# Batch 0 by GpSimd's casting queue, u turned by transposing transfers in five batches, and a new order of the whole list

## The chip, the cores and the metric

The kernel runs on one core of a Trainium2 chip. The metric is the device time of one execution in microseconds. Before the change the median of three runs is 213.06 us (212.74 to 214.03).

## What is computed

The program joins two blocks. The first is a linear attention per head, with a norm over the head's 64 columns; the second mixes tokens and channels with a phase.

```python
kv  = einsum('bhsd,bhse->bhde', k, v)          # 8 batches, 8 heads, 576 rows, 64 columns
o   = einsum('bhsd,bhde->bhse', q, kv)
x   = o / sqrt(mean(o*o, -1) + 1e-6) * g_norm   # then [batch, 576, 512]
th  = x @ w_theta
y   = w_tok_r @ (x * cos(th)) + w_tok_i @ (x * sin(th))
u   = x + y
out = u + maximum(u @ w_ch, 0)                  # float32, 8 x 576 x 512
```

## The kernel before, in words

Each batch has 576 rows. Four tiles of 128 rows (the index j from 0 to 3, called full) and a tail of 64 rows (j = 4, called half-size) make one batch; where a tail is worked on, the two halves of its 512 columns lie on the two halves of the partitions, so it is a tile of 128 x 256. Everything that goes into a matmul is f16, everything that comes out is f32 in PSUM.

`plan()` writes down all tasks of the eight batches. The string `TURNS` is an order over them: each number is a task, and the engines get their instructions in just this order. A letter behind a number moves the task to another engine (A is ACT, D is DVE). A word like `f14` puts 14 filling transposes ahead of the next tile of PSUM, `r20` puts 20 idle matmuls there. Since each engine takes its instructions in order, a task that waits holds up all that stands behind it on its engine, and this is so for the queues of transfers that SP and POOL issue.

For one batch the tasks are these, with the engine that mostly has them:

- `ldm`, `ldt` load k and v (the full rows, the tails), `lq`, `lqe` load q. From batch 1 on they go by POOL's queue, whose transfers turn f32 into f16 on the way, into one of three buffers for each of k, v and q. Batch 0's k and v go as f32 into two buffers of their own (`stage`), k by SP's queue and v by ACT's, in halves of four heads. Two `hold` instructions (L329) on POOL copy one number out of these, so that POOL issues q and the weights only after they are in. `kv_of` (L273) says which buffers a batch uses.
- `kv` (PE), `ko` (ACT or DVE): the 64 x 64 products of k and v, copied into a block-diagonal tile `kbd`.
- q must be turned. For batches 0 and 1 and for all tails `qt` does it on PE and `qo` copies the result out of PSUM; for the full tiles of batches 2 to 7 `qd` (L396) does it by a transposing transfer that SP issues, two for each batch, each from 128 x 1024 to 128 x 8 x 128.
- `raw` (PE) multiplies; `sq` (ACT), `ss` (DVE) and `rt` (POOL, a power of -0.5, L444) make the norm; `x` (DVE) applies it.
- `xt` (PE), `xo` (mostly ACT) turn x; `th` (PE) makes the angle. `pt` (ACT), `arg` (DVE, L511) reduce it to one period, `abs` (DVE, L518) takes its absolute value, `sin` and `cos` (ACT, L526 and L532) follow; the cosine is the one that reads the absolute value. `z` (DVE) multiplies.
- `y`, `ye` (PE, L565 and L574) mix the tokens over nine blocks of the turned token weights `wT`; `us` (DVE, L579) adds x and leaves u turned, channels on partitions, in one of three parts of `uTb`. The tail has `um`, `ug`, `ute`, `uoe`.
- `v` (PE) multiplies the turned u with `wch`. The last sum needs u with rows on partitions: `ut` (L606) turns each full tile back on PE by four transposes, `uo` (L609) copies it from PSUM into `ur`, and `fin` (DVE, L620) makes u + max(v, 0). `st`, `ste` store it by SP's queue.

The weights come once at the start: `lw`, `lwe` (token weights, both parts into the room that `uTb` takes later), `lwth`, `lwch`; `wt` turns the token weights on PE, `wo` copies them out, `wth` scales w_theta. Before all tasks DVE clears the tails of the buffers for k and v and both `kbd`, POOL makes the identity that PE's idle matmuls and transposes need, and PE runs 20 idle matmuls.

Of the kernel before, what the change touches and what calls it, by code (L numbers as in the profile page):

```python
# [40 lines left out]
def plan():  # L41
# [14 lines left out]
    for hh in range(2):  # L56
        add("lqe", "POOL", 0, hh)
    add("hold", "POOL", "k", 0, 0)
    add("hold", "POOL", "k", 0, HH)
# [5 lines left out]
    add("lwth", "POOL")  # L65
# [7 lines left out]
    for b in range(B):  # L73
        if b:
            for t in "kv":
                add("ldm", LOAD[t], t, b, 0, H)
                add("ldt", LOAD[t], t, b)
            add("lq", "POOL", b, 0, H)
            for hh in range(2):
                add("lqe", "POOL", b, hh)  # L80
# [51 lines left out]
4 1 5 0 2 18 16 17 r20 f3 44 45 3 f4 48 49 46A 47 51 50 11 10 6 7 13 12 f14 52 53D f2 54 55 56 21 19  # L132
9 8 59 66 67D 60 f2 61 73 15 14 180 57 62 63 74D 64 178 179 58 f19 34 38 35 68 39A 69 65 30 31A 70
87 75 f10 80 76 23 81 24A 25D 88D 77 26 22 71 78 72 96 97 27A 181 89 82 98 36 79 105 83 90 37 99 84
91 106D 85 182 184 320 183 92 r1 32 114 107 33D 86 100 123 124D 101 93 115 94 102 28 116 95 29D 103
108 104 125 109 42 40 134 117 126 127 111 129 118 119 43 110 120 121 112 41 122 113 128 185 186 187
136 188 190 130 189 135 f9 191 192 198 139 219 193 194 318 317 322 319 131 199D 141 321 146 144 200
195 201 220 140 205 20 196 149 151 132 133 330 331 202 203 323 206D 197 204 153 207 145 137 212 208
# [6 lines left out]
751 362 291 346 460 349 354 461A 355 273 370 462 293D 371 159 174 169 350 363 365 364 366 356 351  # L145
752 357 278 854 988 586 584 587 855 274 283 386 279 377 372 358 373 387D 374 375 367 288 395 284 465
# [3 lines left out]
298 308 420 502 495 590 482 479 483 419 408 496 591 413 592 487 418 593 503 406 720 718 484 594A 885  # L150
488 504 595 519 411 497 489 505 520D 490 716 498 499 983 510 598 407 416 506 423 424 491 500 599 507
# [544 lines left out]
```

## Time and profile before

| | |
|---|---|
| runs | 212.74, 213.06, 214.03 us |
| the profiled execution | 213.28 us |
| its span, first to last instruction | 211.5 us |
| busy: PE, DVE, ACT, POOL | 193.5, 175.2, 135.7, 112.7 us |
| granted clock of TensorE over the span | 0.992 |
| chain that ended last, by engine | PE 47%, DMA 17%, DVE 11%, ACT 7%, POOL 6% |
| DMA queues, share of 16 engines | POOL's casting queue 60.1%, SP's 27.0%, ACT's 1.8% |
| read from HBM, written to it | 33.10 MB, 9.44 MB |

The table is read with two cautions. The ends of matmuls are modelled, so PE's share says when it had something in flight and not how densely it ran. And the share of an engine over the span mixes three stages: a start in which batch 0 and the weights come in, a middle in which several batches overlap, and an end in which only the last batches' products and stores are left.

### The profile page before, as it was taken

What the parts mean: (1) busy time and instruction counts of PE and PEld (TensorE: products, weight loads), DVE (VectorE), ACT (ScalarE), POOL (GpSimd) and SP (SyncE); (2) the same over time, 40 slices, a digit from 0 to 9 for tenths busy, and PEclk for the clock granted to TensorE, in tenths of its full rate; (3) what the DMA queues carried; (4) which work ended last, traced back from release to release, by engine and by line L of the source; (5) the groups of instructions that cost most, each with busy time, mean ns of one, the idle gap of its engine ahead of it and who ended that gap; (6) DMA issues with size and microseconds to landing.
All of it is one profiled execution on the core that took longest, in us unless ns stands there. A gap on an engine that the chain in (4) does not pass through costs nothing.

```text
span 211.5 us, 4732 instructions
## 1 busy us (share of the span) xinstructions
PE 193.5 (91%) x1838; PEld 110.7 (52%) x1838; DVE 175.2 (83%) x358; ACT 135.7 (64%) x271; POOL 112.7 (53%) x116
## 2 busy tenths in 40 slices
PE   7977899999896999999998989799999999999970
PEld 2555557556444565655564565446555556454530
DVE  7016698978997999999998999989999999786660
ACT  2032999469985799599945898658973984570020
POOL 1299898397595899597393643575237310100010
PEclk9999999999999999999999999999999999999996
DMA  5999999994999999999999996999111042214341
GB/s 160 287 139 271 212 184 182 196 192 82 79 183 156 183 228 170 158 219 193 135 119 219 205 183 136 217 144 153 50 54 50 0 120 67 66 50 132 94 173 52
DMA packets 57702, 31.15 MB, mean 147 GB/s; under 512 B 26832, under 2 KB 53072, under 8 KB 57680
## 3 DMA queue, kind: packets, MB, share of 16 engines
q0 software_dynamic: 35888, 15.88, 60.1%
q1 hardware_dynamic: 20208, 13.80, 27.0%
q10 hardware_dynamic: 1584, 1.18, 1.8%
q8 instruction: 14, 0.23, 0.4%
q14 instruction: 8, 0.07, 0.1%
HBM read 33.10 MB, written 9.44 MB: 201 GB/s over the span
## 4 chain that ended last, share of the span: by engine, by line
PE 47%; DMA 17%; DVE 11%; ACT 7%; issue 7%; POOL 6%; POOLq 0%; DVEq 0%; ACTq 0%
PE y L565 17%; DMA k<-in_k_dram 11%; PE v L483 9%; PE th L483 8%; POOL rt L444 4%; DMA uTb<-in_moe_w_tok_r_dram 4%; PE ups L380 3%; DMA qDD<-qh 3%; PE ye L574 2%; DVE ss L438 2%; PE xps L380 2%; PE raw L409 2%; DVE ot L624 2%; ACT sc L532 1%; PE th L490 1%
## 5 line engine op out<-in xcount | busy, mean ns | idle before, releaser
L444 POOL TENSOR_TENSOR rt<-ss,mhalf 128x8 f32<-128x8 f32 x32 | 53.5, 1674 | 35.7 <-DVE ss L438 35.4
L565 PE MATMUL y<-wT,zm 128*128 128x512 f16 x256 | 62.8, 379 | 0.2 <-DVE ot L624 0.2
L565 PEld LDWEIGHTS <-zm 128*128 128x128 f16 x256 | 23.6, 98 | 23.7 <-issue 0.5
L483 PE MATMUL th<-wth,xTb 128*128 128x512 f16 x128 | 32.2, 379 | 0.1
L483 PE MATMUL v<-wch,uTb 128*128 128x512 f16 x128 | 31.9, 379 | 0.0
L429 ACT ACTIVATE sqb<-raw 128x512 f32<-128x512 f32 x32 | 19.1, 598 | 13.9 <-PE raw L409 13.7
L579 DVE SCALAR_TENSOR_TENSOR uTb<-y,gcol,xTb 128x512 f16<-128x512 f32 x32 | 23.4, 743 | 3.0 <-PE y L565 2.9
L438 DVE TENSOR_REDUCE ss<-sqb 128x8 f32<-128x520 f32 x32 | 21.9, 686 | 4.0 <-ACT sqb L429 4.0
L265 ACT COPY ur<-ups 128x512 f16<-128x512 f16 x28 | 16.2, 585 | 13.8 <-PE ups L380 13.8
L526 ACT ACTIVATE sc<-arg 128x512 f16<-128x512 f32 x32 | 20.2, 632 | 6.6 <-DVE arg L511 6.5
L532 ACT ACTIVATE sc<-arg,quarter 128x512 f16<-128x512 f32 x32 | 22.7, 719 | 2.5 <-DVE arg L518 2.5
L456 DVE TENSOR_TENSOR x<-raw,rt 128x512 f16<-128x512 f32 x32 | 21.9, 683 | 2.9 <-POOL rt L444 2.6
L506 ACT ACTIVATE pt<-th 128x512 f32<-128x512 f32 x32 | 18.9, 599 | 7.9 <-PE th L483 7.6
L593 POOL TENSOR_TENSOR uge<-ue,g 128x256 f32<-128x256 f16 x8 | 5.9, 736 | 32.6 <-DVE ue L587 32.6
L624 DVE SCALAR_TENSOR_TENSOR ot<-v,ur 128x512 f32<-128x512 f32 x32 | 21.6, 682 | 1.9 <-PE v L483 1.2
L511 DVE SCALAR_TENSOR_TENSOR arg<-pt,th 128x512 f32<-128x512 f32 x32 | 21.4, 679 | 1.9 <-ACT pt L506 1.7
L540 DVE TENSOR_TENSOR zm<-x,sc 128x1024 f16<-128x1024 f16 x32 | 22.0, 696 | 0.5 <-ACT sc L532 0.4
L267 ACT ACTIVATE xTb<-xps,gcol 128x512 f16<-128x512 f16 x23 | 15.6, 686 | 3.4 <-PE xps L380 3.0
L265 ACT CAST kbd<-kv 64x256 f16<-64x256 f32 (+1 forms) x28 | 9.6, 343 | 12.4 <-PE kv L363 11.1
L483 PEld LDWEIGHTS <-xTb 128*128 128x128 f16 x128 | 11.5, 97 | 11.5 <-issue 0.6
L483 PEld LDWEIGHTS <-uTb 128*128 128x128 f16 x128 | 11.4, 98 | 10.0 <-issue 0.6
L444 POOL TENSOR_TENSOR rte<-sse,mhalf 128x4 f32<-128x4 f32 x8 | 8.6, 1073 | 12.1 <-DVE sse L438 12.1
(101 smaller groups left out, 321.9 us busy)
## 6 DMA issues: line engine op xcount, KB each, us to landing
out_dram<-ot SPq DMA_DIRECT2D x32, 256.0 KB, 2.5
v<-in_v_dram POOLq DMA_DIRECT2D x7, 512.0 KB, 8.6
k<-in_k_dram POOLq DMA_DIRECT2D x7, 512.0 KB, 9.3
qh<-in_q_dram POOLq DMA_DIRECT2D x7, 512.0 KB, 8.6
stage<-in_v_dram ACTq DMA_DIRECT2D x2, 512.0 KB, 8.6
stage<-in_k_dram SPq DMA_DIRECT2D x2, 512.0 KB, 5.4
zm<-in_moe_w_theta_dram POOLq DMA_DIRECT2D x1, 1024.0 KB, 10.3
out_dram<-ote SPq DMA_DIRECT2D x8, 128.0 KB
```

The source lines that it names most:

```text
L265: nc.scalar.copy(out=dst, in_=src)
L438: nc.vector.reduce_sum(out=ss[:], in_=live.pop(("sq", b, j))[:], axis=AXX)
L444: nc.gpsimd.tensor_tensor(out=rt[:], in0=live.pop(("ss", b, j))[:], in1=mhalf[:, 0:h], op=ALU.pow)
L456: nc.vector.tensor_tensor(out=live["xp", b, p][:, :, a * HC:(a + 1) * HC].rearrange("p t (h e) -> p h t e", e=D), in0=r[:].rearrange("p (h ...
L483: nc.tensor.matmul(t[:], lhs(kc), w[:, kc, :], start=(kc == 0), stop=(kc == NKC - 1))
L511: nc.vector.scalar_tensor_tensor(out=arg[:, 0, :], in0=live.pop(("pt", b, j))[:], scalar=MAGIC, in1=live.pop(("th", b, j))[:], op0=ALU.sub ...
L526: nc.scalar.activation(out=sc[:, 1, :], in_=live["arg", b, j][:, 0, :], func=AFT.Sin, bias=0.0, scale=-TURN * SHRINK,)
L532: nc.scalar.activation(out=live["sc", b, j][:, 0, :], in_=live.pop(("arg", b, j))[:, 1, :], func=AFT.Sin, bias=quarter[:], scale=-TURN * S ...
L540: nc.vector.tensor_tensor(out=zm[b % NZ][:, j, :, :], in0=x.unsqueeze(1).broadcast_to((P, 2, C)), in1=sc[:], op=ALU.mult,)
L565: nc.tensor.matmul(t[:], r[:, c * P:(c + 1) * P], wT[:, w, 0:SM], start=(w == 0), stop=(w == 2 * NJ))
L579: nc.vector.scalar_tensor_tensor(out=uTb[:, b % NUT, c, :].rearrange("p (j t) -> p j t", j=NJ), in0=live.pop(("y", b, c))[:].rearrange("p ...
L624: nc.vector.scalar_tensor_tensor(out=ot[:], in0=live.pop(("v", b, j))[:], scalar=0.0, in1=u[:], op0=ALU.max, op1=ALU.add,)
```

## The change

- Batch 0's k and v come by POOL's casting queue as f16, in the same halves, as the first things that POOL issues; `stage`, SP's and ACT's loads and the `hold` instructions are gone. The identity and the constants of -0.5 become a task (`ident`) that stands behind the first four loads.
- k and v have four buffers each instead of three.
- u of batches 2 to 6 (`UD`) is turned back by transposing transfers that SP issues (`ud`), each for two of the four full tiles, into one of two buffers `urd`; for these batches `ut` and `uo` are gone. `uTb` is laid out by tile first, so that a pair of tiles is one run of 1024 columns. A transfer needs all four `us` of its batch.
- q's tail comes in one transfer for each batch with 64 rows on partitions instead of two on 128; PE turns it by four transposes of 64 rows instead of two of 128.
- ACT can take `abs`. With the new marks in `TURNS` 24 of the 32 full and 4 of the 8 half-size ones are its; in exchange DVE has three more `ko`, six half-size `qo` more and two full ones fewer, and one more of `wo`, `wth`.
- `TURNS` is new from end to end, with 13 idle matmuls at the start instead of 20.

```diff
-NSTG, NKV, NQ, NZ, NXT, NUT = 2, 3, 3, 3, 2, 3
+NSTG, NKV, NQ, NZ, NXT, NUT = 0, 4, 3, 3, 2, 3
+NURD = 2
+UD = (2, 3, 4, 5, 6)
-F32 = (0,)
+F32 = ()
...
-        add("ldm", "SP", "k", 0, lo, HH)
-        add("ldm", "ACT", "v", 0, lo, HH)
-    add("ldt", "SP", "k", 0)
-    add("ldt", "ACT", "v", 0)
+        for t in "kv":
+            add("ldm", LOAD[t], t, 0, lo, HH)
+    for t in "kv":
+        add("ldt", LOAD[t], t, 0)
...
-    add("hold", "POOL", "k", 0, 0)
-    add("hold", "POOL", "k", 0, HH)
+    add("ident", "POOL")
...
-            if j < NJ:
+            if b in UD and j % 2 == 0 and j < NJ:
+                add("ud", "SP", b, j // 2)
+            elif j < NJ and b not in UD:
                 add("ut", "PE", b, j)
                 add("uo", "ACT", b, j)
...
-4 1 5 0 2 18 16 17 r20 f3 44 45 3 f4 48 49 46A 47 51 50 11 10 6 7 13 12 f14 52 53D f2 54 55 56 21 19
+0 5 1 4 9 r13 f2 42 43 44A 15 16 14 19 6 2 3 45 f11 50 7 11 8 10 64 51D f1 52 53 54 f19 46 47 49D 48
...
-    qe = many(NQ, [P, HH, D], FP16, "qe")
+    qe = many(NQ, [TL, H, D], FP16, "qe")
...
-    uTb = const.tile([P, NUT, NKC, SM], FP16, name="uTb")
+    uTb = const.tile([P, NUT, NJ, NKC, P], FP16, name="uTb")
...
-    def e_lqe(eng, b, hh):
-        nc.gpsimd.dma_start(
-            out=qe[b % NQ][hh * TL:(hh + 1) * TL, :, :],
-            in_=q[b, hh * HH:(hh + 1) * HH, SM:S, :].rearrange("h s d -> s h d"),
-        )
+    def e_lqe(eng, b):
+        nc.gpsimd.dma_start(out=qe[b % NQ][:], in_=q[b, :, SM:S, :].rearrange("h s d -> s h d"))
...
+    def e_ident(eng):
+        make_identity(nc, ident)
+        nc.gpsimd.memset(mhalf[:], -0.5)
...
-        else:
-            turned("qps", lambda i: qe[b % NQ][:, 2 * i:2 * i + 2, :], NHP // 2, ("qp", b, j))
+            return
+        t = live["qp", b, j] = bank([P, NHP // 2, P], FP16, "tr", 2, "qps")
+        for i in range(NHP):
+            hh, p = divmod(i, 2)
+            nc.tensor.transpose(
+                t[:, p, hh * TL:(hh + 1) * TL], qe[b % NQ][:, 2 * i:2 * i + 2, :], ident[0:TL, 0:TL]
+            )
...
     def e_abs(eng, b, j):
         arg = live["arg", b, j]
+        if eng == "ACT":
+            nc.scalar.activation(out=arg[:, 1, :], in_=arg[:, 0, :], func=AFT.Abs)
+            return
...
-            out=uTb[:, b % NUT, c, :].rearrange("p (j t) -> p j t", j=NJ),
+            out=uTb[:, b % NUT, :, c, :],
...
+    def e_ud(eng, b, p):
+        src = uTb[:, b % NUT, 2 * p:2 * p + 2, :, :]
+        d = wk("urd", [P, 2 * NKC, P], FP16, NURD)
+        nc.sync.dma_start_transpose(out=d[:], in_=src.rearrange("p j k t -> p (j k t)"))
+        for i in range(2):
+            live["ur", b, 2 * p + i] = d[:, NKC * i:NKC * (i + 1), :].rearrange("p k c -> p (k c)")
```

The order changes everywhere, so three places are shown. The first is POOL's opening; `k_64`, `v_68` and `qh_72` are batch 0's buffers, `uTb` holds the token weights at this time. Before:

```order
masks.py:197 MEMSET ident 128x128
masks.py:199 ISA
masks.py:199 AFFINE_SELECT ident<-ident 128x128
L649 MEMSET mhalf 128x8
L329 COPY gate<-stage_64 1x1 x2
L293 DMA qh_72<-in_q_dram 128x4x256 x2
L311 DMA uTb<-in_moe_w_tok_r_dram 64x576
L305 DMA uTb<-in_moe_w_tok_r_dram 128x2304
```

Now:

```order
L279 DMA k_64<-in_k_dram 128x4x256
L285 DMA v_68<-in_v_dram 64x8x64
L279 DMA v_68<-in_v_dram 128x4x256
L285 DMA k_64<-in_k_dram 64x8x64
masks.py:197 MEMSET ident 128x128
masks.py:199 ISA
masks.py:199 AFFINE_SELECT ident<-ident 128x128
L330 MEMSET mhalf 128x8
L292 DMA qh_72<-in_q_dram 128x4x256
```

The loads of batch 0 have taken the place of the two copies that held POOL, and the identity has moved behind four of them.

The second place is DVE from the last `us` of batch 3 on (the numbers behind a tile's name tell one use from another). Before:

```order
L579 SCALAR_TENSOR_TENSOR uTb_90<-y_2012,gcol_102,xTb1_87 128x512
L511 SCALAR_TENSOR_TENSOR arg_2075<-pt_2073,th_2027 128x512
L540 TENSOR_TENSOR zm1_81<-x_1689,sc_2038 128x1024
L511 SCALAR_TENSOR_TENSOR arg_2119<-pt_2108,th_2047 128x512
L624 SCALAR_TENSOR_TENSOR ot_2121<-v_2068,ur_1808 128x512
L456 TENSOR_TENSOR x_2045<-raw_2007,rt_2110 128x4x2x64
L624 SCALAR_TENSOR_TENSOR ote_2124<-v_2089,uge_2032 128x256
L438 TENSOR_REDUCE ss_2126<-sqb1_97 128x8
L271 TENSOR_SCALAR xTb1_87<-xps_2160,gcol_102 128x512
L518 TENSOR_SCALAR arg_2119<-arg_2119 128x512
L518 TENSOR_SCALAR arg_2075<-arg_2075 128x512
L511 SCALAR_TENSOR_TENSOR arge_2194<-pte_2173,th_2141 128x256
```

Now:

```order
L588 SCALAR_TENSOR_TENSOR uTb_90<-y_1995,gcol_102,xTb1_87 128x4x128
L517 SCALAR_TENSOR_TENSOR arg_2056<-pt_2039,th_2028 128x512
L462 TENSOR_TENSOR x_2073<-raw_2013,rt_2047 128x4x2x64
L517 SCALAR_TENSOR_TENSOR arg_2075<-pt_2070,th_2050 128x512
L444 TENSOR_REDUCE sse_2150<-sqe0_98 128x4
L517 SCALAR_TENSOR_TENSOR arge_2154<-pte_2148,th_2077 128x256
L641 SCALAR_TENSOR_TENSOR ote_2156<-v_2128,uge_2000 128x256
L270 TENSOR_SCALAR xTb1_87<-xps_2065,gcol_102 128x512
L472 TENSOR_TENSOR xe_2165<-raw_2097,rte_2163 128x256
L549 TENSOR_TENSOR zm1_81<-x_1685,sc_2036 128x1024
L444 TENSOR_REDUCE ss_2181<-sqb0_96 128x8
L641 SCALAR_TENSOR_TENSOR ot_2183<-v_2173,urd_2058 128x512
```

The absolute values are gone from this stretch, and the first `fin` of batch 3 (the last row, the one that reads `urd`) stands eleven rows behind the last `us`.

The third is SP's queue around the same transfers. Before (`ote_1988` is the tail of batch 2, `qDD_2201` and `qDD_2285` are q of batch 6, `qDD_2307` is q of batch 7):

```order
L636 DMA out_0_dram<-ote_1988 2x64x256
L630 DMA out_0_dram<-ot_1847 128x512
L630 DMA out_0_dram<-ot_2196 128x512
L399 DMA_TRANSPOSE qDD_2201<-qh0_72 128x8x128
L636 DMA out_0_dram<-ote_2124 2x64x256
L399 DMA_TRANSPOSE qDD_2285<-qh0_72 128x8x128
L630 DMA out_0_dram<-ot_2240 128x512
L630 DMA out_0_dram<-ot_2282 128x512
L399 DMA_TRANSPOSE qDD_2307<-qh1_73 128x8x128
```

Now (`qDD_1808` is q of batch 5, the next two are q of batch 6, `urd` is u of batch 3):

```order
L647 DMA out_0_dram<-ot_1769 128x512
L405 DMA_TRANSPOSE qDD_1808<-qh2_74 128x8x128
L405 DMA_TRANSPOSE qDD_1983<-qh0_72 128x8x128
L405 DMA_TRANSPOSE qDD_1985<-qh0_72 128x8x128
L647 DMA out_0_dram<-ot_1779 128x512
L647 DMA out_0_dram<-ot_1971 128x512
L647 DMA out_0_dram<-ot_1824 128x512
L625 DMA_TRANSPOSE urd_2058<-uTb_90 128x8x128
L625 DMA_TRANSPOSE urd_2116<-uTb_90 128x8x128
L653 DMA out_0_dram<-ote_2156 2x64x256
```

q of batch 6 has moved ahead of stores of batch 2, and the transfers of u of batch 3 stand behind both.

More of the change, by code (lines that the diff above doesn't have):

```diff
@@ L64, in plan @@
         add("lg", "SP", i)
-    add("lwth", "POOL")
+    add("lwth", "POOL", 0, 4)
     add("lwch", "POOL")
@@ L78, in plan @@
             add("lq", "POOL", b, 0, H)
-            for hh in range(2):
-                add("lqe", "POOL", b, hh)
+            add("lqe", "POOL", b)
         n = NHP if b else NHP // 2
@@ L606, in e_ut @@
     def e_ut(eng, b, j):
-        turned("ups", lambda i: uTb[:, b % NUT, i, j * P:(j + 1) * P], NKC, ("up", b, j))
+        turned("ups", lambda i: uTb[:, b % NUT, j, i, :], NKC, ("up", b, j))
     def e_uo(eng, b, j):
@@ L615, in e_v @@
         if full(j):
-            dense(t, lambda kc: uTb[:, b % NUT, kc, j * P:(j + 1) * P], wch)
+            dense(t, lambda kc: uTb[:, b % NUT, j, kc, :], wch)
         else:
@@ L623, in e_fin @@
         u = live.pop(("ur", b, j) if full(j) else ("ug", b))
+        u = u if b in UD and full(j) else u[:]
         nc.vector.scalar_tensor_tensor(
-            out=ot[:], in0=live.pop(("v", b, j))[:], scalar=0.0, in1=u[:],
+            out=ot[:], in0=live.pop(("v", b, j))[:], scalar=0.0, in1=u,
             op0=ALU.max, op1=ALU.add,
```

86 lines of the change are left out of this document (48 added, 38 removed), and 14 rows, old and new, of the table TURNS.

## The prediction, made before the change was run

> **What bounds the kernel now.** I read three views, in this order: the busy times by stretch, the groups of instructions, and the waits with the chain. The profiled execution took 213.28 us, 0.22 above the median of the three runs (213.06); its span is 211.5, so 1.8 us lie around the span. First the stretches (span of the stretch, then busy us and instructions of PE, PEld, DVE, ACT and POOL, the granted clock, the DMA share and GB/s):
>
> ```profile
> 40.00:180.00 140.00, 134.16 (x1290) 76.83 (x1288) 132.08 (x261) 105.57 (x211) 85.57 (x77) 1.00 0.95 143
> 180.00:211.50 31.50, 24.87 (x164) 12.38 (x161) 18.29 (x35) 8.51 (x17) 1.35 (x2) 0.94 0.29 95
> 0.00:40.00 40.00, 34.46 (x388) 21.53 (x389) 24.87 (x64) 21.61 (x43) 25.78 (x37) 1.00 1.18 205
> 30.00:40.00 10.00, 9.86 (x129) 6.36 (x128) 9.18 (x23) 8.41 (x17) 6.33 (x9) 1.00 1.65 182
> 60.00:70.00 10.00, 7.92 (x105) 5.03 (x106) 8.53 (x18) 5.81 (x13) 7.23 (x8) 1.00 1.28 170
> 90.00:100.00 10.00, 10.00 (x75) 5.33 (x70) 9.93 (x19) 9.28 (x20) 8.92 (x10) 1.00 1.20 206
> 110.00:120.00 10.00, 9.23 (x94) 5.08 (x89) 9.18 (x19) 6.68 (x14) 5.45 (x5) 1.00 1.32 200
> ```
>
> The reader is to see two engines side by side. In the 140 us in the middle DVE is busy for 132.08, which is 94%, and PE for 134.16. But a PE row's end is modelled: its matmuls overlap. The transposes' pace in the chain shows it:
>
> ```profile
> 188.41 0.45 PE ups L380 x8
> L380 PE MATMUL ups<-ident,uTb 128*128 128x128 f16 x128 | 11.8, 220 | 0.0
> ```
>
> Eight transposes end to end take 0.45 us, 0.056 each, while the mean of one is 220 ns. So PE's 10.0 of 10 in a stretch hides small gaps that a DVE that is always busy leaves to it; DVE's 9.93 of 10 between 90 and 100 us hides almost none. I take DVE as the engine that sets the beat of the middle. The span is then DVE's 175.2 us of work and 36.3 of idle time: 15.1 in the first 40 us, 7.9 in the middle, 13.2 at the end.
>
> The second view says what this DVE time consists of, and what the same kind of work costs on ACT:
>
> ```profile
> L518 DVE TENSOR_SCALAR arg<-arg 128x512 int32<-128x512 int32 x32 | 13.1, 419 | 0.1
> L518 DVE TENSOR_SCALAR arge<-arge 128x256 int32<-128x256 int32 x8 | 2.4, 294 | 0.0
> 28.45 0.33 DVE arg L518
> L506 ACT ACTIVATE pt<-th 128x512 f32<-128x512 f32 x32 | 18.9, 599 | 7.9 <-PE th L483 7.6
> L265 ACT COPY ur<-ups 128x512 f16<-128x512 f16 x28 | 16.2, 585 | 13.8 <-PE ups L380 13.8
> L269 DVE CAST kbd<-kv 64x256 f16<-64x256 f32 x6 | 2.5, 422 | 1.4 <-ACT kbd L265 1.3
> L269 DVE CAST kbd<-kv 64x128 f16<-64x128 f32 x2 | 0.6, 288 | 8.1 <-ACT kbd L265 8.1
> L269 DVE COPY qD<-qps 128x512 f16<-128x512 f16 x5 | 2.1, 418 | 0.4 <-PE qps L380 0.3
> L271 DVE TENSOR_SCALAR xTe<-xps,gcol 128x256 f16<-128x256 f16 x2 | 0.7, 344 | 0.0
> L269 DVE COPY wT<-wps 128x576 f16<-128x576 f16 x4 | 1.8, 452 | 0.7 <-PE wps L351 0.7
> L271 DVE TENSOR_SCALAR wth<-zm 128x512 f16<-128x512 f32 x2 | 0.8, 422 | 0.1
> L271 DVE TENSOR_SCALAR xTb<-xps,gcol 128x512 f16<-128x512 f16 x9 | 4.3, 477 | 0.4 <-PE xps L380 0.4
> ```
>
> The third view shows where the beat is broken in the middle, and what the start waits for:
>
> ```profile
> PE kv L363 <- DMA k<-in_k_dram: 2.5, 2, 1.9
> 59.25 8.21 DMA k<-in_k_dram
> 107.40 14.96 DMA k<-in_k_dram
> 0.74 0.78 SPq L286 DMA_DIRECT2D stage<-in_k_dram  x1
> 1.46 7.01 PE L643 MATMUL idle<-fill,ident 128*128 128x512 f16 x20 [1.46 <-DVE fill L650]
> 8.57 0.69 PE L363 MATMUL kv<-stage,stage 128*64 128x64 f32 x16
> 9.07 0.41 POOL L329 COPY gate<-stage 1x1 f32<-1x1 f32 x2 [7.70 <-DMA stage<-in_k_dram]
> 9.68 1.73 POOL L293 DMA_DIRECT2D qh<-in_q_dram  x2 [0.21 <-issue]
> 19.82 0.41 PE L349 MATMUL wps<-ident,uTb 128*128 128x128 f16 x4 [1.12 <-DMA uTb<-in_moe_w_tok_r_dram]
> ```
>
> At 59.25 k of batch 3 is issued, it lands 8.21 us later, and PE and DVE are short of work: DVE falls to 8.53 of 10. In the start POOL stands for 7.70 us at the hold instruction, until batch 0 is in, and only then issues q and the weights; the token weights' landing is what PE waits for at 19.82.
>
> **The change part by part.** *Absolute values.* 24 of the 32 full ones and 4 of the 8 half ones go from DVE to ACT: 24 x 0.419 + 4 x 0.294 = 11.2 us off DVE. Onto DVE come, by the new engine marks, one block-diagonal copy of batch 0 (2 x 0.288) and two of later batches (4 x 0.422), six half-size copies of q's tail (no such row on DVE; the half-size xTe row has 0.344, so 6 x 0.344 at most), one wT (0.452) and one wth (0.422) and one full xT copy for a half one (0.477 - 0.344); off it go two full q copies (0.84). Together 2.26 + 2.06 + 0.87 + 0.13 - 0.84 = 4.5, net -6.7 us. Next to each other, DVE's instructions overlap: the chain shows an absolute value taking 0.33 where its mean is 0.419. With 16 instructions fewer I give back 0.7, so **-6.0 us of DVE work**. The bounds: -11.2 if the added copies all fall into DVE's idle time, 0 if DVE does not set the beat.
>
> On ACT the absolute value has no row. The nearest rows are ACT's own passes from 128x512 to f32, 0.599: 24 x 0.6 + 4 x 0.38 = 15.9 us come, and 20 copies of turned u at 0.585 = 11.7 go, with five small copies more that go than come. ACT ends near its 135.7 us; it is busy 105.57 of 140 in the middle, so it has room, and I price this at nothing. If that cover is gone, the 4.2 us of difference are the price. The hand-over from DVE to ACT for the cosine falls away.
>
> *u turned by transfers.* 20 x 4 transposes of 0.056 leave PE: 4.5 us, all in batches 2 to 6. Against that PE turns q's tail by four transposes of 64 rows instead of two of 128, 16 more in all, at most 0.9 us. PE gets 3.6 us less to do; while DVE sets the beat, this is not added. Ten transfers come, of the shape that q already has (256 KB, the same instruction):
>
> ```profile
> L399 SPq DMA_TRANSPOSE qDD<-qh x12: 1232/1442/2971, 45.0 to 135.4; - x12
> DMA to landing us min/median/max: 3.9/4.7/8.9
> DMA  5999999994999999999999996999111042214341
> L438 DVE TENSOR_REDUCE sse<-sqe 128x4 f32<-128x260 f32 x8 | 3.4, 420 | 0.6 <-ACT sqe L429 0.6
> L511 DVE SCALAR_TENSOR_TENSOR arge<-pte,th 128x256 f32<-128x256 f32 x8 | 3.3, 410 | 0.0
> L456 DVE TENSOR_TENSOR x<-raw,rt 128x512 f16<-128x512 f32 x32 | 21.9, 683 | 2.9 <-POOL rt L444 2.6
> L540 DVE TENSOR_TENSOR zm<-x,sc 128x1024 f16<-128x1024 f16 x32 | 22.0, 696 | 0.5 <-ACT sc L532 0.4
> ```
>
> A transfer of u can start when the last of the four sums of its batch (e_us) is done on DVE. In the new order (batch 3, shown above) ten instructions stand on DVE between that sum and the first fin that reads the turned u: five full ones (0.68 to 0.70 each) and five near 0.42 to 0.48, 5.6 us by their means, 4.9 after 0.07 of overlap each. The transfer lands in 4.7 at the median. So it is hidden, but by 0.2 us only; the second one is issued 1.4 us later and is read two fins (1.4 us) later. I charge 0.2 us for each of five batches, **+1.0**. Bounds: 0, if all land in 3.9, and 5 x (8.9 - 4.9) = 20 at the longest landing. I stay at the median, since those twelve ran between 45 and 135 us with loads and stores beside them, as batches 2 to 4 will; when batches 5 and 6 turn, few loads are left, as the page's tenths of DMA share show from the 29th slice on (148 us). SP's queue is in order: in batch 3 the transfers stand behind those of q of batch 6 and three stores, which wait for q's load; if that is late, u is late next, then fin, then the stores.
>
> *Batch 0 through the casting queue.* The stretch from 30 to 40 us has that queue nearly alone, at 182 GB/s written. k and v of batch 0 are 1.18 MB as f16, so 1.18 / 0.182 = 6.5 us. The queue can start when SP did, at 0.74 instead of 9.68, so 8.9 us earlier; everything behind batch 0 lands 8.9 - 6.5 = 2.4 us earlier. Batch 0's own first halves are no later: k and v with both tails are 0.66 MB, 3.6 us of that queue. The identity now comes after four issues on POOL (two of 0.94, two near 0.7), so PE's warm-up, which needs it, starts 3.3 us later, near 4.8; 13 idle matmuls at the 7.01 / 20 of the row take 4.6, so the first kv runs near 9.4 instead of 8.57, and gives that much of the gain back. DVE also gets 2 us of added copies in this stage. I take **-2.0** for the start, with bounds 0 (POOL's chain of powers decides) and -2.4.
>
> *Four buffers for k and v, and the order.* The load of k of batch 3 stood behind the first power of batch 2 on POOL; now it is issued before it, and into a buffer of its own. The stretch from 60 to 70 us has 1.47 us of DVE idle time and 1.9 of PE's wait; I take **-1.5**, bounds 0 and -2.7 (the 1.9, and the 0.82 that DVE idles from 110 to 120 us, under the load of k of batch 6). *q's tail in one transfer* takes eight issues from POOL, the loads of batch 0 bring six; POOL is no term.
>
> Sum: 211.5 - 6.0 + 1.0 - 2.0 - 1.5 = 203.0 us of span, 204.8 with the 1.8 around it, **204.6** at the median's level. That is 4.0% faster.
>
> **The rivals.** *PE sets the beat.* For it: 10.0 of 10 in most stretches. Against it: the 0.056 pace, and PE rows that are short of work whenever DVE is. Then -6.0 is replaced by PE's -3.6, the 1.9 of its wait counts, and the start gives nothing: 211.5 - 5.5 = 206.0, so **207.6**.
>
> *The opening starves the queue.* DVE clears buffers while POOL now issues its first loads:
>
> ```profile
> L656 DVE MEMSET k<- 64x256 uint32 x3 | 0.8, 272 | 0.0
> L658 DVE MEMSET kbd<- 128x512 uint32 x2 | 1.0, 485 | 0.2 <-issue 0.2
> L280 POOL DMA_DIRECT2D k<-in_k_dram x7 | 6.6, 940 | 0.0
> ```
>
> The new kernel has eight tail clearings (0.272), two of kbd and one of the filler (0.485): 3.6 us from about 0.9 us on. If POOL's transfers cannot start beside them, the first loads come 3.6 us later: 204.6 + 3.6 = **208.2**. Against it: POOL takes 0.94 to issue a load while DVE is 94% busy, and took 0.87 at 9.68 with DVE idle. The Trainium skill, page "SBUF — State Buffer", section "SBUF: two separate sides", says that while VectorE runs an instruction in a two-port mode, GpSimd is locked out and cannot write the descriptors of its own transfers; by that rule this rival is the outcome, and no run here has yet shown such transfers beside clearings.
>
> *The loads pay.* Ten more transfers share the DMA engines with the casting queue. k of batch 6 took 14.96 us beside two transfers of q and the stores, 6.75 more than k of batch 3. If one load on the path is late by this, it ends at 204.6 + 6.8 = **211.4**, no change.
>
> *u comes late in every batch* (the slower side). SP's order and the traffic make a transfer land at the longest seen, 8.9: DVE stands at fin for 4.0 us in five batches, 19 more than charged, **223.6**. It decides from a mean landing of 6.6 us, where the 8.5 us of gain are gone, and is slower by 1% from 7.0. For it: one transfer of q landed at 8.9, and fin is in order with all else on DVE. Against it: the median of 4.7.
>
> **How the numbers follow.** DVE sets the beat, 204.6: 0.55. PE sets it: 0.18. Starved opening: 0.08. Loads pay: 0.11. u late: 0.08. The first three are faster by over 1% (below 210.9; 1% is about what a measurement of this kernel can tell from no change): 0.81; the fourth lies within: 0.11; the fifth is slower: 0.08. The likeliest one's own range is 201.5 to 208. The range of 200.0 to 212.0 reaches down to the case that the bounds of gain come together (start -2.4, buffers -2.7, and 8 of DVE's 11.2) and up over the loads' case; it leaves out u late and a little on each side.
>
> **What would show it.** Right, if DVE's busy time falls to about 169 us, stays near 94% between 40 and 170 us, the wait of kv for k is gone, the token weights land near 17.5 us, fin waits for urd for under 2 us in all, and ACT stays near 136. Wrong, if DVE falls in share while PE or ACT does not (PE's beat), if the first load's landing is over 7 us (starved), if kv or raw wait for loads for over 5 us, or if urd's median landing is over 6.6 with fin standing behind it.

## The result, and the profile after

The changed kernel takes 222.28 us (median of 4 runs, 221.06 to 223.06), the kernel before 213.22 on the same chip: a ratio of 1.0415, 95% interval 1.0356 to 1.0475. It is slower by 4%, where 4% faster was forecast. The profiled execution took 221.93 us; its span is 220.2, so 1.7 us lie around it, about as before (1.8).

The stretches of the changed kernel, in the columns of those of before:

```profile
0.00:40.00 40.00, 29.85 (x338) 19.02 (x339) 26.38 (x68) 19.89 (x39) 31.21 (x43) 1.00 1.26 177
40.00:100.00 60.00, 59.20 (x596) 34.20 (x594) 57.42 (x111) 48.77 (x98) 44.79 (x41) 1.00 1.36 182
100.00:110.00 10.00, 6.38 (x25) 2.54 (x24) 5.26 (x12) 4.28 (x9) 4.90 (x4) 0.83 1.38 160
110.00:120.00 10.00, 7.00 (x91) 4.87 (x89) 5.94 (x13) 3.29 (x7) 2.42 (x3) 0.83 1.49 135
120.00:130.00 10.00, 5.04 (x24) 2.66 (x24) 3.21 (x6) 2.60 (x6) 2.31 (x2) 0.66 1.05 163
130.00:170.00 40.00, 39.79 (x377) 21.96 (x376) 37.72 (x73) 35.08 (x73) 19.57 (x15) 1.00 0.66 112
sum 222.00, PE 190.13 PEld 106.81 DVE 170.35 ACT 135.08 POOL 111.81; mean PE 27.16 PEld 15.26 DVE 24.34 ACT 19.30 POOL 15.97
```

The same two stretches of the kernel before:

```profile
40.00:100.00 60.00, 56.99 (x561) 32.91 (x559) 55.49 (x108) 47.39 (x96) 48.63 (x49) 1.00 1.23 168
100.00:130.00 30.00, 28.57 (x307) 16.74 (x306) 28.85 (x59) 23.10 (x49) 16.37 (x15) 1.00 1.16 174
```

The reader is to see three things. DVE's and ACT's sums are as forecast (170.3 and 135.1; about 169 and 136 were). Between 40 and 100 us both PE and DVE are fuller than before. And all of the loss lies between 100 and 130 us: DVE works for 14.41 us there (5.26 + 5.94 + 3.21) against 28.85, so 14.4 us of work are missing, while the engines for data are no less busy than before (share 1.05 to 1.49 against 1.16; packets of one engine overlap, so a share can pass 1). In step with this, the first power (`rt`) of batch 4 ends at 94.5 us against 97.5 before, 3 us ahead, and the first of batch 5 at 128.8 against 118.9, 10 behind.

Who waits, of the changed kernel (waits of all engines; sum, times, longest):

```profile
DVE ss L444 <- ACT sqb L435: 9.3, 5, 5.7
PEld L415 <- DMA qDD<-qh: 5.5, 1, 5.5
DVE ot L641 <- DMA urd<-uTb: 5.4, 2, 4.6
PE raw L415 <- DMA qDD<-qh: 5.0, 1, 5.0
DVE ot L641 <- DMA out_dram<-ot: 3.9, 2, 3.5
PE y L574 <- DVE ot L641: 3.6, 1, 3.6
```

The chain through the bad stretch (start, us, what):

```profile
95.20 0.75 DVE uTb L588
95.97 9.75 DMA urd<-uTb
105.80 0.70 DVE ot L641
106.55 4.26 PE y L574 x14
110.81 14.22 DMA qDD<-qh
125.08 0.61 PE raw L415 x4
```

SP's queue there (start, us in all until the last of the group is issued, kind, tiles, count):

```profile
95.97 6.47 SPq L625 DMA_TRANSPOSE urd<-uTb  x2
102.49 0.57 SPq L653 DMA_DIRECT2D out_dram<-ote  x1
103.16 2.35 SPq L647 DMA_DIRECT2D out_dram<-ot  x1
105.62 4.43 SPq L405 DMA_TRANSPOSE qDD<-qh  x1
110.14 0.58 SPq L647 DMA_DIRECT2D out_dram<-ot  x1
110.81 13.90 SPq L405 DMA_TRANSPOSE qDD<-qh  x3
```

Two transfers fill 24 of the 29 us from 95.97 to 125.08: u of batch 2, issued at once when its last sum is done, lands 9.75 us later; then q of batch 5, whose load had landed at 100.5 but whose second transposing transfer is issued only at 110.81, since it stands on SP behind u, the tail's store (`ote`) and other stores, lands after 14.22. PE's `raw` stands for it, ACT and DVE behind PE. The wait of `kv` for k is gone, as forecast. And u does not come late in most batches:

```profile
L625 SPq DMA_TRANSPOSE urd<-uTb x10: 1231/1286/4883, 96.0 to 200.3; - x10
DMA to landing us min/median/max: 3.1/4.0/9.4
```

The count of ten stands for the issues. The trace has the landing of five of them, with a median of 4.0 us, below the 4.7 that the prediction used. Long ones are batch 2's two (9.75 for the first by the chain, 9.4 for the second) and, with 5.5, one of batch 5.

Inside the stretch the two-us windows show what the transfers do:

```profile
104.00:106.00 2.00, 0.00 (x0) 0.00 (x0) 0.20 (x1) 0.34 (x1) 0.00 (x0) 0.94 1.40 138
106.00:108.00 2.00, 1.45 (x4) 0.56 (x4) 2.00 (x4) 0.00 (x0) 0.00 (x0) 0.50 1.44 204
110.00:112.00 2.00, 2.00 (x19) 0.87 (x18) 0.91 (x2) 1.03 (x2) 1.39 (x2) 1.00 3.30 109
112.00:114.00 2.00, 0.16 (x10) 0.07 (x5) 0.00 (x0) 0.70 (x2) 0.00 (x0) 1.00 0.15 34
```

From 112 to 114 us DVE and PE stand, and only 34 GB/s of packets begin. The share of 0.15 does not mean that the engines for data are free: the view counts a packet in the window in which it begins, and the 3.30 of the window before holds packets that run on. By the packets in the trace, 26 that begin between 110.8 and 111.2 us take 3.0 to 3.3 us each, where the median of such packets is 0.06, and all of them end by 114.2. They belong to the transposition of q (256 bytes) and to the loads (512 bytes). What moves meanwhile are the packets of 1024 bytes of the tail's store, which SP issued at 102.49 and whose outermost dimension is two (2x64x256): 128 packets from 106.6 to 112.7 us, some 20 to 22 in each us. The tail's store before it, issued at 87.85, does the same: its last packet ends at 100.4, and 17 others, which took 0.9 to 1.7 us, end by 101.9. Both times the standing packets end 1.4 us after the store's last one; why they do is not shown.

The Trainium skill, page "DMA: Bandwidth & Descriptors", section "Why a DMA increments its semaphore by 16 and not by 1", says that the number of engines a transfer uses is the largest up to 16 that divides the sizes of the slowest dimensions of both sides; for this store that is two. The trace does not name the engine of a packet; that the store's packets come in pairs, 0.095 us from pair to pair, fits two engines.

### The profile page after: what moved, and what is told of

Its sections match the earlier page's. It is cut to its first block, busy times and chain, and to the rows that moved or that the text cites. A ratio compares the mean times of both kernels' runs of the same rounds, so it can differ in the third digit from the quotient of the medians.

```text
span 220.2 us, 4458 instructions
## 1 busy us (share of the span) xinstructions
PE 190.1 (86%) x1727; PEld 106.8 (49%) x1727; DVE 170.3 (77%) x342; ACT 135.1 (61%) x267; POOL 111.8 (51%) x112
## 3 DMA queue, kind: packets, MB, share of 16 engines
q0 software_dynamic: 38928, 17.06, 62.7%
## 4 chain that ended last, share of the span: by engine, by line
PE 38%; DVE 23%; DMA 16%; POOL 8%; ACT 7%; issue 4%; POOLq 0%; DVEq 0%; ACTq 0%
PE y L574 18%; PE v L489 7%; DMA qDD<-qh 6%; DMA zm<-in_moe_w_theta_dram 6%; PE th L489 5%; DMA urd<-uTb 4%; POOL rt L450 4%; DVE ss L444 4%; DVE arg L517 3%; DVE zm L549 3%; DVE x L462 3%; DVE uTb L588 2%; PE ye L583 2%; DVE ot L641 2%; PE raw L415 2%
## 5 line engine op out<-in xcount | busy, mean ns | idle before, releaser
L574 PE MATMUL y<-wT,zm 128*128 128x512 f16 x256 | 64.7, 389 | 3.7 <-DVE ot L641 3.6
L574 PEld LDWEIGHTS <-zm 128*128 128x128 f16 x256 | 24.3, 100 | 29.9 <-issue 7.1
L489 PE MATMUL th<-wth,xTb 128*128 128x512 f16 x128 | 33.1, 383 | 0.5 <-ACT xTb L266 0.4
L641 DVE SCALAR_TENSOR_TENSOR ot<-v,urd 128x512 f32<-128x512 f32 x20 | 13.5, 687 | 9.7 <-DMA urd<-uTb 5.4
L489 PEld LDWEIGHTS <-uTb 128*128 128x128 f16 x128 | 12.1, 100 | 12.1 <-issue 0.7
L450 POOL TENSOR_TENSOR rte<-sse,mhalf 128x4 f32<-128x4 f32 x8 | 8.1, 1012 | 15.5 <-DVE sse L444 15.4
L264 ACT CAST kbd<-kv 64x256 f16<-64x256 f32 (+1 forms) x22 | 7.7, 348 | 12.8 <-PE kv L364 8.9
L525 ACT ACTIVATE arg<-arg 128x512 f32<-128x512 f32 x24 | 15.0, 630 | 0.6 <-DVE arg L517 0.6
## 6 DMA issues: line engine op xcount, KB each, us to landing
uTb<-in_moe_w_tok_r_dram POOLq DMA_DIRECT2D x1, 576.0 KB, 10.3
```

Of the source, the lines that this page charges most:

```text
L450: nc.gpsimd.tensor_tensor(out=rt[:], in0=live.pop(("ss", b, j))[:], in1=mhalf[:, 0:h], op=ALU.pow)
L489: nc.tensor.matmul(t[:], lhs(kc), w[:, kc, :], start=(kc == 0), stop=(kc == NKC - 1))
L574: nc.tensor.matmul(t[:], r[:, c * P:(c + 1) * P], wT[:, w, 0:SM], start=(w == 0), stop=(w == 2 * NJ))
```

## The experiments

The questions are which transfer holds the others up, whether it is one or several, and what each other term of the sum was worth. The times of all runs, each with its ratio to the kernel before run beside it (the names are explained below):

| kernel | median us | ratio, 95% | DVE busy in 100 to 130 us |
|---|---|---|---|
| before | 213.22 | | 28.85 |
| after | 222.28 | 1.0415, 1.0356 to 1.0475 | 14.41 |
| e1: after, store split | 214.98 | 1.0063, 1.0031 to 1.0095 | 19.50 |
| e2: before, store split | 210.42 | 0.9868, 0.9808 to 0.9928 | 29.02 |
| e3: after, store by ACT | 218.02 | 1.0230, 1.0162 to 1.0298 | 17.81 |
| e4: after, u on PE | 224.90 | 1.0530, 1.0466 to 1.0595 | 20.03 |
| e5: e1, u on PE | 215.75 | 1.0104, 1.0054 to 1.0153 | 23.97 |
| e6: e1, k of batch 7 later | 214.80 | 1.0052, 1.0018 to 1.0086 | 17.06 |
| e7: e2, 28 abs on ACT | 217.24 | 1.0156, 1.0114 to 1.0198 | 27.00 |
| e8: e2, batch 0 by POOL | 211.95 | 0.9908, 0.9873 to 0.9944 | 29.06 |
| e9: e1, all abs on DVE | 220.44 | 1.0310, 1.0257 to 1.0362 | 22.66 |
| e10: e1, loads of batch 6 later | 218.38 | 1.0193, 1.0115 to 1.0270 | 23.28 |
| e11: e1, q of batch 5 on PE | 210.22 | 0.9872, 0.9822 to 0.9923 | 23.31 |
| e12: e11, u of batch 2 on PE | 209.35 | 0.9801, 0.9771 to 0.9830 | 23.95 |
| e13: e12, k of batch 7 later | 208.49 | 0.9788, 0.9749 to 0.9826 | 25.63 |

Two theories stood at the start. A: the tail's store, on a few engines, is what the transfers behind it wait for. B: transposing transfers are slow whenever casting loads run beside them, and the ten added ones are too many. The expectations name a third, C: the order on SP's queue alone makes q late. From e10 on they call this one O, and C is there the company of the loads.

**e1, the store in two transfers of 64 partitions each,** so that the slowest dimension is 64:

```diff
-        queue[eng].dma_start(
-            out=out[b, SM:S, :].rearrange("s (hh c) -> hh s c", hh=2), in_=live["ot", b, NJ][:]
-        )
+        for hh in range(2):
+            queue[eng].dma_start(
+                out=out[b, SM:S, hh * HC:(hh + 1) * HC],
+                in_=live["ot", b, NJ][hh * TL:(hh + 1) * TL, :],
+            )
```

> The changed kernel, with the store of each batch's tail as two transfers of 64 partitions instead of one of 2 x 64 rows. Theory A (the tail's store runs at 20 KB/us at a DMA share of 0.07, one engine of 16, for some 6 us, and every load and turn that has a part on that engine lands late): the stall between 100 and 130 us goes, DVE is over 9 of 10 there, the time is 203 to 210 us. Theory B (transposing transfers are slow whenever casting loads run beside them, and ten more of them are too many): nothing changes, 219 to 224 us. Theory C (SP's queue issues u of batch 2 ahead of q of batch 5, so order alone makes q late): nothing changes either, 219 to 224 us.

**e2, the same edit in the kernel before.**

> The kernel before, with the same split of the tail's store. Theory A: its two slow landings (k of batch 6 with 15 us, q turned for batch 5 with 5.5 on the chain) get shorter too, 208 to 212 us. Theories B and C: 213, no change; the 8 more issues on SP cost nothing.

**e3, the store unchanged, but issued by ACT** (`nc.scalar.dma_start` in place of SP's queue).

> The changed kernel, with the tail's store in its old form but issued by ACT's queue. Theory A in the form that the one engine is the straggler for all: still slow, 216 to 222 us, and k's loads and u's turns land as late as before. Theory A in the form that only what stands behind the store in SP's own queue waits: the stall goes, 204 to 211 us (ACT pays some 0.5 us for each of eight issues). Theories B and C: 219 to 224 us.

**e4, no transposing transfer for u:** `ud` is taken out, and where it stood PE turns u of batches 2 to 6 by 16 transposes for a batch, and ACT copies:

```diff
-    def e_ud(eng, b, p):
...
+    def e_turn(b, j):
+        turned("ups", lambda i: uTb[:, b % NUT, j, i, :], NKC, ("up", b, j))
+        d = wk("urq", [P, C], FP16, 6)
+        copy_out("ACT", d[:], live.pop(("up", b, j))[:].rearrange("p k c -> p (k c)"))
+        live["ur", b, j] = d[:]
```

> The changed kernel without the ten transposing transfers: u of batches 2 to 6 turned on PE near the place where the transfer was issued, and copied out by ACT into six buffers. PE does 4.5 us more, ACT 11.7. Theory B: the stall between 100 and 130 goes since only q's transfers are left, 205 to 210 us. Theory C: the same, since u no longer stands ahead of q. Theory A: part of the stall stays, since the tail's store still holds up q's turn and k: 209 to 216 us.

e1 takes 7.5 us off (1.0415 to 1.0063 of 213), e3 takes 3.9 off, e4 takes nothing off and lies outside all that was expected of it. So the store costs 7.5 us, a little over half of it because it is issued on SP's queue, the rest wherever it is issued. In e1 the long packets are gone with it: none of those two sizes that begins from 95 to 116 us takes more than 0.41, and the store's own packets are through in 0.6 us (105.8 to 106.4). That the ten transfers alone are the loss, as theory B has it, is not borne out; but e4 also gives PE and ACT the work of turning u, and its stretch from 100 to 130 us does fill to 20.03, so it does not clear these transfers. And e2 shows that the store is not the change's own: it was in the kernel before as well and cost 2.8 us there, so 4.7 of the 7.5 are what the new order adds. With the store split in both, the changed kernel is still 4.2 us slower (1.0063 against 0.9868). So e1 is no whole answer, and DVE still has only 19.50 of 30 us of work between 100 and 130. Its chain, and the landings of q's transfers in the same time:

```profile
96.75 8.82 DMA urd<-uTb
106.80 12.99 DMA qDD<-qh
```

```profile
L405 SPq DMA_TRANSPOSE qDD<-qh x4: 1244/2470/4390, 103.7 to 117.8; - x4
DMA to landing us min/median/max: 4.8/7.7/13.0
```

**e5, e4's edit on top of e1; e6, one load moved on top of e1,** to tell two theories apart: T, that u's transfers hold q up; L, that the loads come in the wrong order (k of batch 7 is loaded at 80 us ahead of all of batch 5). The row of e6 in POOL's order:

```diff
-ldm(k,4,0,8) lq(4,0,8) ldt(v,7) rt(3,0) rt(3,1) ldm(k,7,0,8) ldt(k,7) rt(3,3)
+ldm(k,4,0,8) lq(4,0,8) ldt(v,7) rt(3,0) rt(3,1) rt(3,3)
...
-lq(6,0,8) rt(4,3) ldm(k,6,0,8) rt(4,4)
+lq(6,0,8) rt(4,3) ldm(k,6,0,8) ldm(k,7,0,8) ldt(k,7) rt(4,4)
```

> The changed kernel with the tail's store in two transfers, and u of batches 2 to 6 turned on TensorE and copied by ACT again, as in batches 0, 1 and 7 (no transposing transfer for u at all). With the two-part store alone it took 214.98 us and was still slow from 100 to 120 us, where two transposing transfers of u, issued at 96.75, land after 8.8 us and q of batch 5 stands behind them on SP's queue. Theory T (with the store out of the way, the transposing transfers of u are what holds q up between 100 and 120): that stretch fills, the time falls by 5 us or more, to 207 to 210 us. Theory L (loads that run in another order come in late, transfers of u are only in their company): 213 to 216 us, with q of batch 5 late as before. Under both, TensorE gets 4.5 us of work back.

> The changed kernel with the tail's store in two transfers and one load moved in GpSimd's order: k of batch 7 (main part and tail) behind k of batch 6, where the loads before it (v and q of batch 5, k of batch 5, v, q and k of batch 6) are no longer preceded by it. Theory L (the changed order loads k of batch 7 at 80 us ahead of all of batch 5, which fourth buffers allow, and pushes q of batch 5 back by the 5 to 6 us that a megabyte takes): q of batch 5 lands some 4 to 6 us sooner than 101.3, the stretch from 100 to 120 us shortens by about as much, 208 to 211 us. Theory T (the transposing transfers of u): q may land sooner but its transposing transfers still stand behind those of u; 213 to 216 us.

Both miss the gain that their theory promised: 1.0104 and 1.0052 against e1's 1.0063, no difference that these intervals show. In e5 the stretch fills (23.97), but from 140 to 180 us DVE is at 35.0 of 40 against 38.2 in e1: what is gained in one place is given back over the rest. That the turning of all twenty tiles of u on PE and ACT does this is argued, not shown. In e6 q of batch 5 does land 3 us sooner, at 98.05, and `raw` then waits 8.2 us for its turned form, instead of 3.9 in e1 (e6's row, then e1's):

```profile
PE raw L415 <- DMA qDD<-qh: 8.2, 1, 8.2
PE raw L415 <- DMA qDD<-qh: 3.9, 1, 3.9
```

So neither the number of u's transfers nor the landing of q seems to decide, and the transposing of q itself is left.

**e10 and e11 ask that directly, on top of e1.** e10 moves the three loads of batch 6 out of the way of q's transfers; e11 does without these transfers:

```diff
-rt(4,1) rt(4,2) ldm(v,6,0,8) lq(6,0,8) rt(4,3) ldm(k,6,0,8) rt(4,4) ug(3)
+rt(4,1) rt(4,2) rt(4,3) rt(4,4) ldm(v,6,0,8) lq(6,0,8) ldm(k,6,0,8) ug(3)
```

```diff
+            if word[0] == "Q":
+                b, j = map(int, word[1:].split("."))
+                e_qt("PE", b, j)
+                e_qo("ACT", b, j)
...
-st(1,3) qd(5,1) st(2,3) qd(5,0) qd(6,1) qd(6,0)
+st(1,3) st(2,3) qd(6,1) qd(6,0)
```

> The changed kernel with the tail's store in two transfers (214.98 us by itself) and the three loads of batch 6 (v, q, k) moved in GpSimd's order behind the last normalising pass of batch 4, instead of standing among those passes; nothing else. Theory C (q of batch 5's two transposing transfers, issued at 103.7 and 106.8, are caught in the company of three loads issued at 102.4, 103.4 and 110.2, run at 60 KB per us beside them and land at 114 and 119.8): without that company they land 4 to 6 us after they were issued, TensorE's wait for them goes, 206 to 210 us. Rival O (the order on SP's queue alone: q of batch 5 stands behind two transposing transfers of u, the tail's store and two others): the wait stays, 213 to 216 us. Rival S (batch 6 then starves): the stall moves to 125 to 140 us, 212 to 217 us.

> The changed kernel with the tail's store in two transfers (214.98 us by itself) and q of batch 5 turned on TensorE (16 transposes) and copied by ACT, as in batches 0 and 1, in place of its two transposing transfers; nothing else. If these two transfers are the stall (theories C and O): raw of batch 5 waits for the load of q alone, which landed at 101.3; the stretch 100 to 120 us fills and 206 to 210 us come, with some 2 us more of TensorE and 2.4 of ACT. If the loads themselves are late: 213 to 216 us.

e10 is slower (218.38, above even what was expected if the stall moves), and is still the one that shows the mechanism. The transfers of q of batches 5 and 6 in it, in the same view as e1's:

```profile
L405 SPq DMA_TRANSPOSE qDD<-qh x4: 1232/1302/1311, 103.9 to 124.9; - x4
DMA to landing us min/median/max: 3.2/4.6/5.6
```

The two of batch 5 are issued at 103.90 and 106.31 (103.74 and 106.80 in e1), now without the loads beside them, and land after 4.0 and 3.2 us instead of 10.3 and 13.0; the 5.6 is one of batch 6's. SP's order is unchanged. So the theory that the order on SP's queue alone does it falls, and the company of loads is what makes these transfers slow: the first half of theory B. But then the next transposing transfers, u of batch 3, meet the next loads, q and v of batch 7, and DVE stands there instead. The chain of e10:

```profile
96.78 8.30 DMA urd<-uTb
128.95 7.67 DMA urd<-uTb
```

and its stretches:

```profile
110.00:120.00 10.00, 8.81 (x116) 5.58 (x115) 7.92 (x17) 7.11 (x14) 5.99 (x6) 1.00 0.41 52
130.00:140.00 10.00, 4.75 (x21) 2.02 (x22) 2.36 (x4) 5.07 (x12) 2.54 (x2) 0.82 1.41 204
```

DVE has 7.92 of 10 from 110 to 120 us (6.45 in e1) and 2.36 from 130 to 140 (9.83 in e1). That is the third outcome that was written down beforehand: the stall moves. e11 takes q's two transfers away instead, costs PE 16 transposes and ACT four copies, and gains 4.1 us (1.0063 to 0.9872); at 210.22 it lies just above the 206 to 210 that was expected.

**e12 and e13 go after what is left in e11,** u of batch 2 (issued at 97.44, landing after 8.15 us), and after the order of loads again. e12 uses e4's `e_turn` for batch 2 alone; e13 adds e6's edit.

> The changed kernel with the tail's store in two transfers, q of batch 5 turned on TensorE (210.22 us so far), and now also u of batch 2 turned on TensorE (16 transposes, four copies by ACT) in place of its two transposing transfers. Theory C for the rest (two transposing transfers issued while megabyte loads are in flight come 8 us later, and DVE's first output of batch 2 waits for them): the stretch 100 to 110 us fills, 205.5 to 208 us. If the rest lies elsewhere (TensorE, busy 98 per cent between 40 and 100 us, gets 1 us more work): 209.5 to 212 us.

> As the kernel with q of batch 5 and u of batch 2 on TensorE, and k of batch 7 loaded behind k of batch 6 instead of ahead of all of batch 5. If the loads' order costs anything once the transposing transfers are out of the way (q of batch 5 lands 3 us sooner, at 98): 1.5 to 4 us less than that kernel. If q of batch 5 landing at 101 is early enough: within 1 us of it.

e12 gains 1.5 us more by the ratios (0.9872 to 0.9801; the intervals touch), less than the 2.2 to 4.7 expected of the theory, and nearer to its rival's bounds (209.5 to 212) than to its own. e13 is the same within its interval: the order of loads is worth nothing that can be measured here. Both are faster than the two kernels, than the one before by about 2%.

**e7 and e9 test the term for DVE, e8 that for the opening.** e7 moves the 28 absolute values to ACT in e2's order (28 marks `A` in `TURNS` and ACT's branch of `e_abs`); e9 moves them back to DVE in e1's order (the 28 marks `A` are taken out). e8 is e2 with

```diff
-NSTG, NKV, NQ, NZ, NXT, NUT = 2, 3, 3, 3, 2, 3
+NSTG, NKV, NQ, NZ, NXT, NUT = 0, 3, 3, 3, 2, 3
-F32 = (0,)
+F32 = ()
...
-        add("ldm", "SP", "k", 0, lo, HH)
-        add("ldm", "ACT", "v", 0, lo, HH)
+        add("ldm", "POOL", "k", 0, lo, HH)
+        add("ldm", "POOL", "v", 0, lo, HH)
```

(the tails alike), these loads first in POOL's order, behind the identity, and no `hold`.

> The kernel before with the tail's store in two transfers (210.42 us by itself) and, as the only other edit, the same 28 absolute values on ACT that the change moves there; order and everything else as before. The prediction's term for DVE (DVE sets the beat; 11.2 us of work go from it and nothing comes): 4 to 8 us less, 202 to 206 us. The rival that TensorE sets the beat as well (57.8 of 60 us busy between 40 and 100 us in the same kernel): 0 to 2 us less, 208.5 to 210.5 us. If ACT, which gets 16 us more, comes late for the cosine: more than 211 us.

> The changed kernel with the tail's store in two transfers (214.98 us by itself) and the 28 absolute values that the change moved to ACT back on DVE, at the same places of the order; the only other edit. Moving them the other way in the kernel before cost 3 per cent. The prediction's term for DVE (it sets the beat, so each microsecond on it counts): DVE gets 11.2 us back where it is 95 to 99 per cent busy already, 219 to 223 us. Rival (with absolute value, sine and cosine all on ACT the hand-over to DVE's z comes late, and ACT's 16 us cost as much as they save): 213 to 216 us, no change. If the same move costs here what it cost in the kernel before: below 211 us.

> The kernel before with the tail's store in two transfers (210.42 us by itself) and batch 0's k and v loaded by GpSimd's casting queue in the changed kernel's order, nothing held back, f16 from the start; order otherwise as before. The prediction's term for the opening: 2.0 us less, 208.4 us, with the token weights landed near 17.5. What the changed kernel's trace suggests (its last x of batch 0 ends at 27.2 us against 27.1): no gain, 209.5 to 211.5 us, token weights near 19.6.

e9 loses 5.3 us (1.0310 against 1.0063; by the two intervals 4 to 6.6). e7 loses 6.1 us, where the term for DVE promised a gain of 4 to 8. The same 28 instructions are worth +5.3 us in one order and -6.1 in the other. In the old order, DVE's middle, and a wait that was 0.2 us in e2:

```profile
40.00:180.00 140.00, 131.54 (x1255) 74.58 (x1256) 120.83 (x226) 114.03 (x232) 85.19 (x77) 1.00 0.92 141
```

```profile
DVE zm L542 <- ACT sc L534: 6.0, 9, 1.5
```

DVE is busy for 120.83 of 140 us, against 132.08 in the kernel before, so it did get the time; but it now waits 6.0 us for ACT's sine and cosine, which stand behind the absolute value, and PE falls back with it. The wait is shown; that it makes up all of the 6.1 us is not.

e8 gains nothing: 0.9908 against 0.9868. It is only a rough test, since its opening is poorer than the changed kernel's: the first load lands 7.4 us after its issue instead of 4.6, and the last `x` of batch 0 ends at 29.4 us instead of 27.2.

## Why the prediction was wrong, point by point

**The step that failed is the price of the transposing transfers on SP's queue.** The prediction charged +1.0 us for u's ten, five times 0.2, at the median landing of 4.7, and looked at one wait only, that of `fin`. It put at nothing what the new order does to q's transfers and to the tail's store on the same queue, though it said that u's transfers stand behind q's and that "if that is late, u is late next". The runs show it the other way round, and at another price. q of batch 5 is issued late because u of batch 2, the tail's store and other stores stand ahead of it on SP, and it is then transposed beside three loads; without that company (e10) its two transfers land after 4.0 and 3.2 us instead of 10.3 and 13.0 (e1). What the runs take back by mending these places one after the other: the store 7.5 us (e1), of which 2.8 were in the kernel before as well, q of batch 5 4.1 (e11), u of batch 2 1.5 (e12). That is 10.3 us of the change's own, against 1.0. `fin` waits 5.4 us for u, where under 2 was forecast. How much of the 10.3 is due to u's transfers and how much to the new order around them stays open: e4 and e5 have no transfer of u at all and are no faster.

The landing was taken from too little as well. The 4.7 stands beside twelve transfers, but the trace of the kernel before has the landing of four of them, 4.0, 5.5, 4.0 and 8.9 us, so one in four was at the longest. A median was the wrong number for it: 4.0 came true, and the two transfers of batch 2 that took 9.75 and 9.4 began the loss. And the charge of 0.2 does not follow from its own sum, in which 4.7 is hidden behind 4.9.

**The rivals.** "The loads pay" had the right mechanism, a transposing transfer and the loads sharing the engines, but let it hit a load, once, for 6.8 us; it hit q's and u's transfers. "u comes late in every batch" gave 223.6, next to what was measured, and that is luck: u came late in one batch. The starved opening did not happen in the changed kernel: amid the clearings the first packet of the first load runs 1.7 us after the issue, as long as in the kernel before with DVE idle (issue at 9.68, packet at 11.37), and the load landed 4.6 us after its issue. The rule cited for this rival speaks of instructions in a two-port mode; no run shows that a clearing is one.

**DVE, -6.0.** Its busy time fell to 170.3 as forecast, and e9 gives 5.3 us for the move of the absolute values alone. That this is near 6.0 is no proof of the term: it is the gain for 11.2 us of work that leave DVE, about half a microsecond for each of them, and the copies that came in exchange were not tried by themselves. Nor does it hold just because "DVE sets the beat". In e7's order the same move loses, with DVE waiting for ACT's result. ACT's own row for it was priced at 0.599 and is

```profile
L525 ACT ACTIVATE arg<-arg 128x512 f32<-128x512 f32 x24 | 15.0, 630 | 0.6 <-DVE arg L517 0.6
```

**PE sets the beat** was given 0.18. Between 40 and 100 us of the changed kernel PE is busy for 59.20 of 60 and DVE for 57.42; in e9, where DVE has more to do, PE falls to 56.10 and DVE is at 56.45. So neither is shown to bound the middle alone. That the 5.4 us still missing below are PE's is not shown either.

**The opening, -2.0.** Nothing came. In the changed kernel PE reaches the first token weights at 19.63 us, where 17.5 was forecast and 19.82 was before, and the last `x` of batch 0 ends at 27.2 against 27.1; e8 agrees. The changed kernel's first 10 us:

```profile
0.00:5.00 5.00, 0.00 (x0) 0.00 (x0) 3.69 (x16) 1.49 (x2) 3.88 (x12) 1.00 0.46 51
5.00:10.00 5.00, 4.99 (x12) 1.79 (x13) 0.26 (x2) 0.00 (x0) 4.93 (x9) 1.00 1.32 142
```

The casting queue was taken at 182 GB/s from 0.74 us on. All queues together move 51 GB/s in the first 5 us and 142 in the next 5, 0.97 MB by 10 us where 9.3 x 0.182 = 1.69 was assumed; the 0.73 MB that lack are 4.0 us of that queue, more than the 2.4 of gain. The first packet runs at 2.9 us, so 2.2 of the 4.0 are gone before the queue moves anything. Why it starts so slowly was not tried.

**Four buffers, -1.5.** The wait of `kv` for k is gone, and batch 4 starts 3 us ahead; by then about half of DVE's 6.0 should have come as well, so the two together gave less than their terms. No run separates them.

**The sum.** 204.6 was forecast from a time that had the store's 2.8 us in it. With +10.3 for the transfers and the rest of the store and +2.0 for the opening that gave nothing it comes to 216.9 of the 222.3. 5.4 us are open. The like shows without the sum: e12 has the mended places and is 1.4 us faster than e2, the kernel before with the split store (0.9801 against 0.9868), where the whole change was to give 8.5. Even these 1.4 us lie within the two intervals.

## What to carry to other kernels

A transfer added to an in-order queue is priced by what stands behind it on that queue, and by the loads in flight when it runs, at its longest landing and not its median. Where transposing transfers have to run among large loads, turning on TensorE the q of one batch and the u of another, for which the order waits, was worth 5.6 us here, moving the loads away lost 3, and giving up every transfer of u was worth nothing. An instruction moved between engines is worth what the order makes of it: the same move gained 5.3 us and lost 6.1.

## What the runs showed of the hardware

- A transposing transfer beside casting loads: in e1, by the bytes of the packets in the trace, 56 to 62 KB per us from 109 to 113 us, with 121 to 123 KB per us of casting loads beside it; with nothing beside it, at 121 us, 257 KB in one us. The Trainium skill, page "DMA: Bandwidth & Descriptors", section "Latency and other measured facts", gives 261 GB/s for a transposing transfer with a non-contiguous middle dimension, and about 350 to 400 for a contiguous one. The 257 of the one that runs alone is next to the first figure; which case it is no run here tells. Among loads a quarter of it is left.
- A store of 128 KB whose outermost dimension is two needed 6.1 us for its packets (106.6 to 112.7). Meanwhile 26 packets of loads and of a transposing transfer, issued by POOL and SP, stood for 3.0 to 3.3 us. In two transfers of 64 partitions (e1) the same bytes took 0.6 us and no such packet stood. The store cost 2.8 us in one order and 7.5 in another.
- PE's granted clock falls after PE has stood still: PE waits 3.62 us until 106.55, then the clock is 0.50 from 106 to 108 us and 0.70 from 108 to 110, and 14 matmuls of `y` take 4.26 us, 0.30 each. Elsewhere in the same chain eight take 1.73 us, 0.22 each. So this stall cost about 1.2 us more than its length.
